# The second batch's first groups leave the start of a two-stage FFT and feed-forward kernel; its first pair loads change queues

## The chip, the cores and the metric

The kernel runs on one core of one Trainium2 chip. The metric is the device time of one execution in microseconds (us). A core has five engines with a queue each: TensorE (PE; weight loads are listed as PEld), VectorE (DVE), ScalarE (ACT), GpSimd (POOL) and SyncE (SP), which here only issues transfers. Transfers are issued by SP, ACT and POOL.

## What is computed

```python
X = np.fft.rfft(x, axis=1)                      # x: 4 batches, 3008 rows, 256 columns
Yr = Xr @ w_r - Xi @ w_i + b_r                  # complex mixing, 256 x 256
Yi = Xr @ w_i + Xi @ w_r + b_i
Yr, Yi = soft_threshold(Yr, 0.01), soft_threshold(Yi, 0.01)
y = np.fft.irfft(Yr + 1j * Yi, n=3008, axis=1)
h = y.reshape(12032, 256) @ w_in                # 256 -> 2048
g = np.maximum(h, 0) + alpha * np.minimum(h, 0)
out = g @ w_out                                 # 2048 -> 256
```

## The kernel before

Each of the four batches goes through four steps, and then through the feed-forward layers. **Step A** is the first half of the transform: 16 groups, each one product over 512 columns in full float32 (`a_mm`, L389) and one copy out of PSUM (`a_evac`, L404 and L406). Batch 0's groups stay in SBUF, in `a0_s`. Those of the other batches are stored to a DRAM buffer `ad` (the L336 issues, made by `put`). **Step B** is the second half: 12 pairs. `b_load` fetches a pair with two transfers of 128 KB into a `bt` tile (three of them), `b_mm` (L428) transforms it with the table `rb_s`, `b_evac` and `b_evac2` split it into a high and a low part (`Xh` by ACT L442, `Xl` by DVE L453, copies by POOL L457), and `m_mm` (L471, L478) applies the mixing weights. **Step C** (`m_evac`, `c_mm`, `c_evac`) is the soft threshold and the first half of the inverse transform, and goes to DRAM (`zd`). **Step D** reads it back (`zt`, L584) and finishes the inverse (L620), which feeds the layers (L689, L726 to L728).

The program is one fixed order, written by hand: each engine takes its instructions in the order in which they are issued, and an instruction that has to wait holds up all that stands behind it on its engine. This goes for SP's transfers too.

The start is: step A of batch 0; four groups of batch 1 (`EARLY`); the loads of the first three pairs, the split of the mixing weights (`split_mix`: high part by ACT, low part by POOL) and the bias parts; `keep_warm(70)`, products on a tile of zeros that keep TensorE busy and whose result nobody reads; then the 12 pairs of batch 0. While the pairs run, `pump` converts feed-forward weights to two-part form with ACT, DVE and POOL: `PT` says how many pieces of this work each pair gets, and `conv_load` fetches the raw weights (`cw_s`, 512 KB each). A list `TAIL` then fills the wait for step C's last stores with ten groups of batch 1 (entries `['f', 4]` and `['f', 6]`, limited by `FILL`).

Then the **weight pass** begins: 48 steps, three chunks of rows for each of the 16 blocks of the hidden layer, while the rest of the weights is converted. What else is to run in a step stands in a table, filled by `at(i, fn, ...)`. The groups of batch 1 that are left go there, by these lines:

```python
for g in range(FILL, NG):
    i = 6 * (g - FILL) + 9
    if g % 2 == 0:
        at(i - 8, a_load, 1, g // 2)
    at(i, a_mm, 1, g)
    at(i, a_evac, 1, g)
```

`a_load` fetches the rows of two groups at once. Also in that table: step 40 loads the table `lc_s` (four transfers of 768 KB, by POOL) and the next `zt`, step 45 loads batch 1's first pair from `ad`, and step 49 (just behind the weight pass) transforms it.

Of the kernel before, what the change touches and what calls it, by code (L numbers as in the profile page):

```python
# [93 lines left out]
def fft_mix_moe(ctx, tc, x, w_r, w_i, b_r, b_i, w_in, w_out, alpha, la, rb, lc, rd, lf, cf, sel, out):  # L94
    nc = tc.nc
# [35 lines left out]
    V, G, A, PE = nc.vector, nc.gpsimd, nc.scalar, nc.tensor  # L131

    def f(t):
        return t.bitcast(F32)

    def split(src, hi, lo, e_hi, e_lo):

        if e_hi is A:
            A.activation(out=hi, in_=src, func=AF.Copy)
        else:  # L140
            e_hi.tensor_copy(out=hi, in_=src)
        e_lo.tensor_tensor(out=lo, in0=src, in1=f(hi), op=ALU.subtract)
# [24 lines left out]
    def half(h):  # L167
        t = const.tile([128, 2, FH * 2 * C], F32R, tag=f"half{h}", name=f"w{h}")
        wi_h[h] = t[:, 0].rearrange("p (w k f) -> p w k f", w=2, k=CT)
        wo_h[h] = t[:, 1].rearrange("p (m w f) -> p m w f", w=2, f=C)  # L170

    def load_tables():
        nc.sync.dma_start(out=rd_s, in_=rd)
        nc.sync.dma_start(out=alpha_s, in_=alpha.rearrange("(k p) -> p k", p=128))
# [33 lines left out]
    def load_mix(*tags):  # L208
        for w, tag in zip((w_r, w_i), tags):
            t = work.tile([128, CT, C], F32, tag=tag, name="wm_f", bufs=1 if tag[1] in "tc" else None)  # L210
            nc.sync.dma_start(out=t, in_=w.rearrange("(k p) f -> p k f", p=128))
            mix_w.append(t)

    def load_rb(n0, n1):
        nc.sync.dma_start(out=rb_s[:, n0:n1], in_=rb[:, n0:n1])
# [9 lines left out]

    def split_mix():
        for t, w in zip(mix_w, mix):
            split(t, w[:, 0], w[:, 1], A, G)
        mix_w.clear()

    def combine_mix():
# [17 lines left out]
    conv_tags = {}  # L249
# [4 lines left out]
    def conv_load():  # L254

        m, i = divmod(conv_m[0], 2)
        conv_m[0] += 1
        k = conv_m[0] % 3
        raw = cw_s[:, NSLOT + 8 * k:NSLOT + 8 * k + 8].rearrange("p (k n) f -> p k (n f)", k=2)
        raw = raw.rearrange("p k (n w) -> p k n w", w=2)  # L260
        src = w_out.bitcast(U32)[256 * m:256 * m + 256] if i else w_in.bitcast(U32)[:, 512 * m:512 * m + 512]
        nc.sync.dma_start(out=raw.rearrange("p k n w -> p k (n w)"), in_=src.rearrange("(k p) f -> p k f", p=128))
        conv_raw.append((raw, m, i))
# [70 lines left out]
    def put(*queues):  # L334
        for n, (o, i) in enumerate(stores):
            (queues or (nc.sync,))[n % max(len(queues), 1)].dma_start(out=o, in_=i)  # L336
        stores.clear()
# [3 lines left out]
    def a_load(b, g):  # L341

        if g == 0:
            ad[b] = dram.tile([NQ, R, C], F32, tag="ad", name=f"ad{b}")
        src = x[b].rearrange("(p r) c -> p r c", r=R)[:, 4 * g:4 * g + 4]
        if b == 0:
            ts = [x_s[:, 4 * g:4 * g + 4]]
        elif b == 1 and g in X1_TAGS:
            tags = X1_TAGS[g]
            ts = [work.tile([NP, 4 // len(tags), C], F32, tag=tag, name="xt", bufs={"Yl": None, "gh": 4}.get(tag, 1))  # L350
                  for tag in tags]
        else:
            ts = [work.tile([NP, 4, C], F32, tag="xt", name="xt")]
        if (b, g) == (0, 0):
            ts = [ts[0][:, 0:2], ts[0][:, 2:4]]
        n = 4 // len(ts)
        for i, t in enumerate(ts):

            for p in ((0, 80), (80, NP)):
                nc.sync.dma_start(out=t[slice(*p)], in_=src[slice(*p), n * i:n * i + n])  # L360
        xt[b, g] = ts

    def x_rows(b, g):
        ts = xt[b, g // 2]
        if len(ts) == 1:
            return [ts[0][:, 2 * (g % 2):2 * (g % 2) + 2]]
        n = len(ts) // 2
        return ts[n * (g % 2):n * (g % 2) + n]
# [13 lines left out]
    def a_mm(b, g):  # L382
        ps = ps_f.tile([NQ, 2, C], F32, tag="f", name="ps_a")
        pa[b, g] = ps
        if b < 2:
            ts = x_rows(b, g)
            n = 2 // len(ts)
            for i, t in enumerate(ts):
                PE.matmul(ps[:, n * i:n * i + n], lf_s, t, start=True, stop=True)  # L389
            return  # L390
        hi, lo = xp.pop((b, g))
        PE.matmul(ps, la_s[:, 0], hi, start=True, stop=False)
        PE.matmul(ps, la_s[:, 1], hi, start=False, stop=False)
        PE.matmul(ps, la_s[:, 0], lo, start=False, stop=True)

    def a_evac(b, g):
        ps = pa.pop((b, g))
        if b == 0:
            st = a0_s[:, g]
        else:  # L400
            tag = A1_TAGS[g] if b == 1 and g < len(A1_TAGS) else "zst"
            st = work.tile([NQ, 2, C], F32, tag=tag, name="ast", bufs={"bt": 3, "zst": 3, "Yt": 1, "Yc": 1}.get(tag))
        if b == 0 and g % 2:
            V.tensor_copy(out=st, in_=ps)  # L404
        else:
            A.activation(out=st, in_=ps, func=AF.Copy)  # L406
        if b:
            stores.append((ad[b][:, 2 * g:2 * g + 2], st))

    bt, xs, xe, yc, ys = {}, {}, {}, {}, {}  # L410

    def b_load(b, q):
        t = work.tile([128, 2, C], F32, tag="bt", name="bt", bufs=3)
        if b == 0:
            src = a0_s.rearrange("(w s q) g r c -> q w s (g r) c", w=4, s=2)[q]
        else:
            src = ad[b].rearrange("(w s q) r c -> q w s r c", w=4, s=2)[q]

        for k in range(2):
            (nc.gpsimd if b == 0 else nc.sync).dma_start(out=t[:, k], in_=src[:, k])  # L420
        bt[b, q] = t

    def b_mm(b, q):
# [548 lines left out]
    MM, M2 = 2, 4  # L972
    PAT = [0, 0] + [1] * 46
    NG = R // 2
    EARLY = 4
    FILL = 14
    C0 = 2
    PT = [1, 2, 3, 3, 3, 3, 3, 3, 3, 3, 4, 4]
    TAIL = [['me', 1], ['ce', 3], ['cm', 2], ['cm', 1], ['ce', 2], ['ce', 1], ['d'], ['f', 4], ['e'], ['f', 6]]
    WARM = 70  # L980
    A1_TAGS = ("zst", "zst", "Yt", "Yc", "bt", "bt", "bt", "Xh", "Xl", "Xh", "Xl", "zst", "zst", "Yc")
    X1_TAGS = {4: ("Yl", "Yl"), 5: ("os", "Yt"), 6: ("gh",) * 4}
    idle = const.tile([128, 128], BF16, name="idle")

    def keep_warm(n):
        ps = ps_f.tile([128, 512], F32, tag="f", name="ps_idle")
        for _ in range(n):
            PE.matmul(ps[:, 0:128], idle, idle, start=True, stop=True)

    with tc.manual_schedule():  # L990
        V.memset(idle, 0.0)
        nc.gpsimd.dma_start(out=lf_s, in_=lf)
        bias_parts = first_bias()
# [2 lines left out]
        for g in range(NG // 2):  # L996
            a_load(0, g)
        load_rb(0, 4)
        for g in range(EARLY // 2):
            a_load(1, g)  # L1000
        load_mix("Yh", "Yh")
        load_rb(4, 12)
        conv_tags.update(v1=("yh", "yl"), ex=("xh", "xh"), lf=("xl", "xl"))
        for _ in range(C0):
            conv_load()
        seq = [(0, g) for g in range(NG)] + [(1, g) for g in range(EARLY)]

        for n, (b, g) in enumerate(seq):
            a_mm(b, g)
            if n >= 1:  # L1010
                a_evac(*seq[n - 1])
            if n == NG:
                for q in range(3):
                    b_load(0, q)
                split_mix()
                bias_parts()
        a_evac(*seq[-1])
        half(0)
        put()
        load_tables()  # L1020
        keep_warm(WARM)

        def run(fn, q, *args):
            if 0 <= q < NPAIR:
                fn(0, q, *args)

        a1 = [EARLY]
        hold = []

        def a_fill(n):  # L1030
            for g in range(a1[0], min(a1[0] + n, FILL)):
                a_mm(1, g)
                a_evac(1, g)
                a1[0] = g + 1

        for t in range(NPAIR + 1):
            run(b_mm, t)
            run(b_load, t + 3)
            run(c_evac, t - 4)
            run(b_evac, t)  # L1040
            run(m_evac, t - 2)
            run(m_mm, t - 1, ps_h)
            run(b_evac2, t)
            run(c_mm, t - 3)
            if t < NPAIR:
                pump(PT[min(t, len(PT) - 1)])
            if t in (2, 5):
                load_rb(2 * t + 8, 2 * t + 14)
            if t < 8 and t % 2 == 0:
                load_cf(3 * t, 3 * t + 6)  # L1050
            if 5 <= t < 10:
                a_load(1, t - 3)
            if t == 10:
                half(1)
                conv_m[1] = FT
# [46 lines left out]
        for b in range(B):  # L1102
# [9 lines left out]
            if b == 0:  # L1112
# [3 lines that stand above are left out]
# [84 lines left out]
        for k in range(len(spairs) + SLAG):  # L1200
# [9 lines left out]
            if k >= SLAG:  # L1210
                n, t = spairs[k - SLAG]
# [43 lines left out]
```

## Time and profile before

| | |
|---|---|
| time, median of 3 runs | 1350.1 us (1348.96 to 1350.62) |
| the profiled execution: its own time | 1350.56 us |
| the profiled execution: span from the first to the last instruction | 1348.8 us |
| TensorE busy | 1335.5 us (99% of the span), 9200 matmul records |
| VectorE, ScalarE, GpSimd busy | 1034.9, 761.0, 375.5 us |
| granted TensorE clock, mean | 0.999 of full speed |

The busy time of TensorE counts the products on zeros as well, so "99% busy" doesn't mean that 99% is useful. A full-float32 product shows as two matmul records. Each view below has the start of an instruction or of a run of instructions in us from the span's start, then its duration.

### The profile page before, as it was taken

Reading aid. Unit: us, or ns where it says so; the run is one execution under the profiler, and the core shown is the slowest. Engines: PE = TensorE matmul, PEld = TensorE weight load, DVE = VectorE, ACT = ScalarE, POOL = GpSimd, SP = SyncE. Lnnn points to the kernel's source line nnn. Section 1 sums busy time; section 2 is a strip of 40 time slices with the busy share of each in tenths; the row PEclk is TensorE's granted clock in tenths of the full one; section 3 lists DMA queues with packets and bytes.
Section 4 is the critical chain, followed back from the end, with each engine's and each line's share of the span. In section 5 each row is a group of like instructions: output and inputs, shape, how many; then the busy total and the mean of one; then the engine's idle time right before and its main releaser. Section 6 shows DMA issues by size and latency. Waiting matters only on the chain.

```text
span 1348.8 us, 25138 instructions
## 1 busy us (share of the span) xinstructions
PE 1335.5 (99%) x9200; PEld 1250.7 (93%) x9200; DVE 1034.9 (77%) x1938; ACT 761.0 (56%) x1526; POOL 375.5 (28%) x400
## 2 busy tenths in 40 slices
PE   8999999999999999999999999999999999999998
PEld 4979999999999999999999999999999999999998
DVE  2767856776777777776768888888888888888885
ACT  3566655665566645555555555655555555555653
POOL 3864642222321222222221211121112111211222
PEclk9999999999999999999999999999999999999999
DMA  9974223342333312111110110111011101110001
GB/s 236 251 202 140 81 94 106 105 138 74 98 115 112 111 54 79 53 51 47 36 36 2 40 28 4 37 28 28 6 35 28 28 6 35 29 28 8 22 17 29
DMA packets 88119, 89.67 MB, mean 66 GB/s; under 512 B 42317, under 2 KB 70448, under 8 KB 87995
## 3 DMA queue, kind: packets, MB, share of 16 engines
q1 hardware_dynamic: 79700, 77.02, 20.1%
q0 software_dynamic: 5168, 8.02, 2.2%
q10 hardware_dynamic: 3127, 3.01, 0.7%
q8 instruction: 73, 1.20, 0.4%
q14 instruction: 51, 0.42, 0.1%
HBM read 50.49 MB, written 34.34 MB: 63 GB/s over the span
## 4 chain that ended last, share of the span: by engine, by line
PE 89%; DVE 3%; DMA 3%; issue 2%; ACT 1%; SPq 1%; POOL 0%; ACTq 0%; DVEq 0%; POOLq 0%
PE ps_h L794 24%; PE ps_h L689 13%; PE ps_m L491 6%; PE ps_o L895 6%; PE ps_o L896 6%; PE ps_o L894 6%; PE ps_d L620 4%; PE ps_o L728 3%; PE ps_o L727 3%; PE ps_o L726 3%; PE ps_b L428 2%; PE o_last L727 1%; PE o_last L728 1%; PE o_last L726 1%; PE o_last L894 1%
## 5 line engine op out<-in xcount | busy, mean ns | idle before, releaser
L794 PE MATMUL ps_h<-yh,w 128*128 128x512 f32 (+1 forms) x960 | 315.6, 389 | 0.0
L833 POOL TENSOR_TENSOR l<-t,h 128x512 fp32r<-128x512 f32 x98 | 127.0, 1296 | 496.5 <-ACT h L831 456.9
L794 PEld LDWEIGHTS ps_h<-yh,w 128*128 128x128 f32 x960 | 180.0, 188 | 33.2
L798 DVE SCALAR_TENSOR_TENSOR sq<-sq,beta_s,ps_h 128x512 f32<-128x512 f32 (+1 forms) x240 | 167.9, 732 | 54.5 <-ACT sq L797 53.6
L689 PE MATMUL ps_h<-yh,w 128*128 128x384 f32 (+1 forms) x704 | 207.0, 337 | 1.3 <-DVE q L696 1.3
L794 PE MATMUL ps_h<-yl,w 128*128 128x512 f32 (+1 forms) x480 | 186.2, 388 | 0.0
L696 DVE SCALAR_TENSOR_TENSOR q<-q,beta_s,ps_h 128x384 f32<-128x384 f32 (+1 forms) x192 | 115.1, 600 | 91.8 <-ACT q L695 90.9
L700 ACT ACTIVATE gh<-q 128x384 fp32r<-128x384 f32 (+1 forms) x192 | 99.1, 516 | 148.0 <-DVE q L696 145.3
L701 POOL TENSOR_TENSOR gl<-q,gh 128x384 fp32r<-128x384 f32 (+1 forms) x90 | 96.8, 1075 | 274.9 <-ACT gh L700 265.4
L813 ACT ACTIVATE dh<-sq 128x768 fp32r<-128x768 f32 x112 | 94.8, 846 | 117.8 <-DVE sq L798 75.8
L797 ACT ACTIVATE sq<-ps_h 128x512 f32<-128x512 f32 (+1 forms) x240 | 133.2, 586 | 26.9 <-PE ps_h L794 25.6
L689 PEld LDWEIGHTS ps_h<-yh,w 128*128 128x128 f32 x704 | 129.3, 189 | 4.4 <-DVE q L696 1.3
L695 ACT ACTIVATE q<-ps_h 128x384 f32<-128x384 f32 (+1 forms) x192 | 91.9, 479 | 62.1 <-PE ps_h L689 61.4
L831 ACT ACTIVATE h<-t 128x512 fp32r<-128x512 f32 x98 | 62.0, 633 | 105.2 <-DVE t L829 103.0
L689 PE MATMUL ps_h<-yl,w 128*128 128x384 f32 (+1 forms) x352 | 116.5, 331 | 0.0
L728 PE MATMUL ps_o<-w,gl 128*128 128x256 f32 x384 | 108.0, 281 | 0.6 <-POOL gl L701 0.6
L727 PE MATMUL ps_o<-w,gh 128*128 128x256 f32 x384 | 107.8, 281 | 0.0
L726 PE MATMUL ps_o<-w,gh 128*128 128x256 f32 x384 | 107.7, 280 | 0.0
L794 PEld LDWEIGHTS ps_h<-yl,w 128*128 128x128 f32 x480 | 90.5, 189 | 13.6
L828 DVE TENSOR_TENSOR dl<-sq,dh 128x768 fp32r<-128x768 f32 x98 | 93.4, 953 | 3.9 <-ACT dh L813 3.9
L896 PE MATMUL ps_o<-l,sw_a 128*128 128x256 f32 x294 | 82.0, 279 | 0.0
L894 PE MATMUL ps_o<-h,sw_a 128*128 128x256 f32 x294 | 81.9, 279 | 0.0
(214 smaller groups left out, 3618.5 us busy)
## 6 DMA issues: line engine op xcount, KB each, us to landing
zt<-zd SPq DMA_DIRECT2D x32, 384.0 KB
zd<-zst SPq DMA_DIRECT2D x37, 256.0 KB
ad<-ast SPq DMA_DIRECT2D x48, 192.0 KB
bt<-ad SPq DMA_DIRECT2D x72, 128.0 KB
xt<-in_x SPq DMA_DIRECT2D x21, 320.0 KB
out<-oT SPq DMA_DIRECT2D x152, 32.0 KB
cw_s<-in_moe_w_in SPq DMA_DIRECT2D x8, 512.0 KB
cw_s<-in_moe_w_out SPq DMA_DIRECT2D x8, 512.0 KB
```

The lines of the kernel that those rows point to most:

```text
L689: PE.matmul(ps, wi_h[m // FH][:, w, ct, 128 * (m % FH):128 * (m % FH) + 128], a[:, ct, 0:n], start=(k == 0), stop=(k == 3 * CT - 1))
L696: V.scalar_tensor_tensor(out=q, in0=q, scalar=beta_s[:, m:m + 1], in1=ps, op0=ALU.mult, op1=ALU.add)
L700: A.activation(out=hi, in_=q, func=AF.Copy)
L726: PE.matmul(a, hi[:, t], w[:, 0], start=(i, k) in first, stop=False)
L727: PE.matmul(a, hi[:, t], w[:, 1], start=False, stop=False)
L728: PE.matmul(a, lo[:, t], w[:, 0], start=False, stop=(i, k) in last)
L794: PE.matmul(ps, wi_h[m // FH][:, w, ct, 128 * (m % FH):128 * (m % FH) + 128], a[:, ct, 0:w1], start=(k == 0), stop=(k == 3 * CT - 1))
L797: A.activation(out=q[:, j], in_=ps, func=AF.Relu, scale=-1.0)
L798: V.scalar_tensor_tensor(out=q[:, j], in0=q[:, j], scalar=beta_s[:, m:m + 1], in1=ps, op0=ALU.mult, op1=ALU.add)
L833: G.tensor_tensor(out=l24, in0=t24, in1=f(h24), op=ALU.subtract)
L894: PE.matmul(o, wh, gh, start=first, stop=False)
L896: PE.matmul(o, wh, gl, start=False, stop=last)
```

## The change

The four early groups of batch 1 are dropped from the start, and with them the loads of their rows and the stores of their results. The tail still does ten groups, now groups 0 to 9 and not 4 to 13; six groups (10 to 15) and not two are left for the weight pass, at steps 9, 15, 21, 27, 33 and 39 and not at 9 and 15. The rows for the tail's groups load with pairs 7 to 11 and not 5 to 9 (and so with two earlier loads). Pairs 0 and 1 of batch 0 are loaded half by SP and half by ACT, ahead of `rb_s` and the raw weights; pair 2 and later ones stay with POOL. The low part of the mixing weights is split by DVE and not by POOL. The two small tables `rd_s` and `alpha_s` load with pair 6 and not before pair 0. `keep_warm(70)` becomes `keep_warm(56)`, and 12 such products come ahead of pair 1. `PT` starts with one piece less in pairs 0 and 1, and has one more in pairs 8 and 9.

```diff
-            split(t, w[:, 0], w[:, 1], A, G)
+            split(t, w[:, 0], w[:, 1], A, V)
...
-    def b_load(b, q):
+    def b_load(b, q, queues=None):
+        queues = queues or ((nc.sync,) * 2 if b else (nc.gpsimd,) * 2)
...
-            (nc.gpsimd if b == 0 else nc.sync).dma_start(out=t[:, k], in_=src[:, k])
+            queues[k].dma_start(out=t[:, k], in_=src[:, k])
...
-    EARLY = 4
-    FILL = 14
+    FILL = 10
-    PT = [1, 2, 3, 3, 3, 3, 3, 3, 3, 3, 4, 4]
+    PT = [0, 1, 3, 3, 3, 3, 3, 3, 4, 4, 4, 4]
-    WARM = 70
+    WARM = 56
...
-        for g in range(EARLY // 2):
-            a_load(1, g)
         load_mix("Yh", "Yh")
+        for g in range(NG):
+            a_mm(0, g)
+            if g:
+                a_evac(0, g - 1)
+        a_evac(0, NG - 1)
+        both = nc.sync, nc.scalar
+        b_load(0, 0, both)
+        b_load(0, 1, both)
         load_rb(4, 12)
+        b_load(0, 2)
         for _ in range(C0):
             conv_load()
-        seq = [(0, g) for g in range(NG)] + [(1, g) for g in range(EARLY)]
...
+        bias_parts()
+        split_mix()
         half(0)
-        put()
-        load_tables()
         keep_warm(WARM)
...
         for t in range(NPAIR + 1):
+            if t == 1:
+                keep_warm(12)
...
-            if 5 <= t < 10:
-                a_load(1, t - 3)
+            if 7 <= t < 12:
+                a_load(1, t - 7)
+            if t == 6:
+                load_tables()
```

SP's queue at the start, behind the last rows of batch 0 (`xt` are rows of batch 1, `wm_f` the mixing weights, `bt<-a_83` halves of pairs 0 and 1, `ad_160` the early groups' stores):

```order
 L215 DMA rb_s<-tab_rb 128x512
-L360 DMA xt<-in_x 80x1024
-L360 DMA xt<-in_x 14x1024
-L360 DMA xt<-in_x 80x1024
-L360 DMA xt<-in_x 14x1024
 L211 DMA wm_f<-in_w_r 128x2x256
 L211 DMA wm_f<-in_w_i 128x2x256
+L421 DMA bt<-a_83 128x1x256 x2
 L215 DMA rb_s<-tab_rb 128x1024
 L262 DMA cw_s<-in_moe_w_in 128x2x512
 L262 DMA cw_s<-in_moe_w_out 128x2x512
-L336 DMA ad_160<-ast 96x512 x4
```

The rows of batch 1 and the stores are gone, and SP's halves of pairs 0 and 1 stand ahead of `rb_s` and of two raw weights.

TensorE's queue in the weight pass at the end of step 21, before the change:

```order
L726 MATMUL ps_o<-w_255,gh 128x256
L727 MATMUL ps_o<-w_255,gh 128x256
L728 MATMUL ps_o<-w_255,gl 128x256
L689 MATMUL ps_h<-Xh,w_255 128x384
L689 MATMUL ps_h<-Xl,w_255 128x384
```

The same place with the change (lines below the new one in the file moved down by one):

```order
L727 MATMUL ps_o<-w_232,gh 128x256
L728 MATMUL ps_o<-w_232,gh 128x256
L729 MATMUL ps_o<-w_232,gl 128x256
L389 MATMUL ps_a<-xt,lf_s 96x512
L690 MATMUL ps_h<-Xh,w_232 128x384
L690 MATMUL ps_h<-Xl,w_232 128x384
```

One group of step A stands between the second layer's products of one step and the first layer's of the next; so it is at steps 27, 33 and 39 too.

SP's queue ahead of batch 1's first pair (`bt<-ad`), before the change, from the last store of a group (`ad_160<-ast`) on:

```order
L336 DMA ad_160<-ast 96x512
L262 DMA cw_s<-in_moe_w_in 128x2x512
L262 DMA cw_s<-in_moe_w_out 128x2x512
L211 DMA wm_f<-in_w_r 128x2x256
L211 DMA wm_f<-in_w_i 128x2x256
L181 DMA bias<-in_b_r 128x256
L181 DMA bias<-in_b_i 128x256
L584 DMA zt<-zd_495 96x1024
L420 DMA bt<-ad_160 128x1x256 x2
```

And with the change:

```order
L336 DMA ad_719<-ast 96x512 x2
L211 DMA wm_f<-in_w_r 128x2x256
L211 DMA wm_f<-in_w_i 128x2x256
L181 DMA bias<-in_b_r 128x256
L181 DMA bias<-in_b_i 128x256
L336 DMA ad_719<-ast 96x512
L585 DMA zt<-zd_460 96x1024
L421 DMA bt<-ad_719 128x1x256 x2
```

The last store, that of step 39's group, now stands directly ahead of the `zt` load for step 45 and of batch 1's first pair.

## Rows read from the trace of the kernel before

**Rows 1.** The page: busy us, share of the span and records of each engine.
```profile
PE 1335.5 (99%) x9200; PEld 1250.7 (93%) x9200; DVE 1034.9 (77%) x1938; ACT 761.0 (56%) x1526; POOL 375.5 (28%) x400
```

**Rows 2.** Timeline of TensorE, start: start us, duration us, instructions, idle before.
```profile
25.52 4.07 PE L988 MATMUL ps_idle<-idle 128*128 128x128 bf16 x70
30.42 1.80 PE L428 MATMUL ps_b<-rb_s,bt 128*128 128x128 f32 x12 [0.83 <-issue]
...
33.56 0.47 PE L471 MATMUL ps_m<-bias_p,ones 128*128 128x512 f32 x1
...
36.72 1.05 PE L428 MATMUL ps_b<-rb_s,bt 128*128 128x128 f32 x8
```

**Rows 3.** Timeline of the other engines around the first pair loads.
```profile
19.94 0.69 DVE L404 COPY a<-ps_a 96x512 f32<-96x512 f32 x1 [1.03 <-PE ps_a L389]
...
20.27 0.37 SPq L262 DMA_DIRECT2D cw_s<-in_moe_w_out  x1
...
21.29 4.11 POOL L420 DMA_DIRECT2D bt<-a  x6 [16.19 <-DVE bias_h L201]
```

**Rows 4.** Tile `bt`, issue to landing: the load issued at 21.3, then 18 to 60 us.
```profile
DMA to landing us min/median/max: 9.0/9.0/9.0
...
DMA to landing us min/median/max: 4.2/8.5/9.9
```

**Rows 5.** Transfers of the first 100 us: issues, KB each, us from issue to landing.
```profile
lf_s<-tab_lf POOLq DMA_DIRECT2D x1, 35.2 KB, 2.9
```

**Rows 6.** Chain of work that ended last, in order of time: start, duration, what.
```profile
17.30 6.10 DMA wm_f<-in_w_i
...
92.09 8.59 PE ps_a L389 x24
...
206.56 0.89 PE ps_b L428 x8
```

**Rows 7.** Stages: length, busy time of PE, PEld, DVE, ACT, POOL, clock, DMA, GB/s.
```profile
4.70:20.70 16.00, 14.81 (x36) 5.03 (x34) 5.56 (x11) 4.74 (x8) 0.40 (x1) 1.00 1.06 231
20.70:25.50 4.80, 3.69 (x8) 1.19 (x9) 1.15 (x3) 2.71 (x5) 4.11 (x6) 1.00 1.07 356
...
50.00:70.00 20.00, 20.00 (x153) 19.25 (x152) 17.34 (x23) 11.94 (x22) 19.30 (x24) 1.00 1.03 278
```

**Rows 8.** Timelines: `Xl` of pairs 10 and 11 on VectorE, its first use on TensorE.
```profile
79.19 0.67 DVE L453 TENSOR_TENSOR Xl<-ps_b,Xh 128x512 fp32r<-128x512 f32 x1
...
84.50 0.68 DVE L453 TENSOR_TENSOR Xl<-ps_b,Xh 128x512 fp32r<-128x512 f32 x1
...
79.54 1.05 PE L428 MATMUL ps_b<-rb_s,bt 128*128 128x128 f32 x8
...
74.70 1.05 PE L428 MATMUL ps_b<-rb_s,bt 128*128 128x128 f32 x8
...
85.23 0.39 PE L478 MATMUL ps_m<-wr_s,Xl 128*128 128x256 f32 x1
```

**Rows 9.** Timeline of SP: the last row loads of batch 1 with pair 9.
```profile
70.24 9.29 SPq L360 DMA_DIRECT2D xt<-in_x  x12
```

**Rows 10.** Timeline of TensorE in the weight pass: its idle gaps from 150 us on.
```profile
151.15 0.44 PE L689 MATMUL ps_h<-Xh,w 128*128 128x384 f32 x1 [0.38 <-DVE q L696]
...
159.71 0.44 PE L689 MATMUL ps_h<-yh,w 128*128 128x384 f32 x1 [0.39 <-DVE q L696]
...
168.99 0.39 PE L728 MATMUL ps_o<-w,gl 128*128 128x256 f32 x1 [0.62 <-POOL gl L701]
```

**Rows 11.** A stage behind these gaps (columns as in rows 7).
```profile
170.00:180.00 10.00, 10.00 (x75) 10.00 (x74) 6.09 (x12) 5.23 (x13) 5.29 (x4) 1.00 0.00 0
```

**Rows 12.** Tile `ast`, 100 to 150 us: ScalarE's copies, ns min/median/max.
```profile
L406 ACT ACTIVATE ast<-ps_a x4: 576/586/594, 99.9 to 138.0; 96x512 f32<-96x512 f32 x4
```

**Rows 13.** Timelines of SP and GpSimd ahead of batch 1's first pair.
```profile
149.30 1.28 SPq L420 DMA_DIRECT2D bt<-ad  x2
...
187.41 2.96 POOL L224 DMA_DIRECT2D lc_s<-tab_lc  x4
```

More of the change, by code (lines that the diff above doesn't have):

```diff
@@ L974, in fft_mix_moe @@
     NG = R // 2
-    EARLY = 4
-    FILL = 14
+    FILL = 10
     C0 = 2
-    PT = [1, 2, 3, 3, 3, 3, 3, 3, 3, 3, 4, 4]
+    PT = [0, 1, 3, 3, 3, 3, 3, 3, 4, 4, 4, 4]
     TAIL = [['me', 1], ['ce', 3], ['cm', 2], ['cm', 1], ['ce', 2], ['ce', 1], ['d'], ['f', 4], ['e'], ['f', 6]]
-    WARM = 70
-    A1_TAGS = ("zst", "zst", "Yt", "Yc", "bt", "bt", "bt", "Xh", "Xl", "Xh", "Xl", "zst", "zst", "Yc")
-    X1_TAGS = {4: ("Yl", "Yl"), 5: ("os", "Yt"), 6: ("gh",) * 4}
+    WARM = 56
+    A1_TAGS = ("bt", "bt", "bt", "Xh", "Xl", "Xh", "Xl", "zst", "zst", "Yc")
+    X1_TAGS = {2: ("Yl", "Yl"), 3: ("os", "Yt"), 4: ("gh",) * 4}
     idle = const.tile([128, 128], BF16, name="idle")
@@ L998, in fft_mix_moe @@
         load_rb(0, 4)
-        for g in range(EARLY // 2):
-            a_load(1, g)
         load_mix("Yh", "Yh")
+        conv_tags.update(v1=("yh", "yl"), ex=("xh", "xh"), lf=("xl", "xl"))
+        for g in range(NG):
[6 more added lines that the diff above has]
+        b_load(0, 1, both)
         load_rb(4, 12)
-        conv_tags.update(v1=("yh", "yl"), ex=("xh", "xh"), lf=("xl", "xl"))
+        b_load(0, 2)
         for _ in range(C0):
             conv_load()
-        seq = [(0, g) for g in range(NG)] + [(1, g) for g in range(EARLY)]
[L1008 to L1017, printed above, removed]
+        bias_parts()
+        split_mix()
         half(0)
-        put()
-        load_tables()
         keep_warm(WARM)
@@ L1025, in run @@
                 fn(0, q, *args)
-        a1 = [EARLY]
+        a1 = [0]
         hold = []
```

## The prediction

> **What bounds the kernel now.** I read the page first: TensorE is busy for 1335.5 us of the span of 1348.8 us [rows 1], so the time is TensorE's own work plus its gaps. The change removes no useful product. It can pay only by shortening the time in which TensorE does nothing useful, and the page hides the largest such place, since products on zeros count as busy. The timeline of TensorE at the start shows it: between the four early groups of batch 1 and pair 0 stand 4.07 us of products on zeros, the first pair's transform comes only at 30.42, and the first mixing product at 33.56 [rows 2]. Once the pairs run TensorE has no gap (20.00 us busy of 50 to 70, at a granted clock of 1.00 [rows 7]), so what is won ahead of 33.56 moves all that follows, unless a later stage gives it back.
>
> What holds back 30.42? The last group of step A is out of PSUM at 19.94 + 0.69 = 20.63, and GpSimd issues six loads from 21.29 on [rows 3]. The first landed 9.0 us later [rows 4], at 30.3. So the wait is for pair 0's load. That load was behind others: a 512 KB raw weight was issued one microsecond ahead [rows 3], the mixing weight landed at 17.30 + 6.10 = 23.40 [rows 6], and the transfer engines were busy throughout (share 1.07 [rows 7]).
>
> **Pairs 0 and 1 by SP and ScalarE, and nothing ahead of them.** They can be issued at 20.63. The rows of batch 1 (two loads of 384 KB, 768 KB) no longer stand ahead of the mixing weights; at the 231 GB/s of that stage [rows 7] this is 3.3 us, so the weights land at about 20.1 and the queue is then empty. `rb_s` and the raw weights are issued behind. How long a load of this kind takes from these queues no row shows. From below: a 35 KB load by GpSimd into a quiet chip took 2.9 us [rows 5]. From above: 9.0 us as now. The two halves of a pair bring 256 KB, 0.7 us at 356 GB/s [rows 7]. As the queue is empty I take the near end, 3.4 us: pair 0's transform starts at 24.0. The 56 products on zeros end before that (from 19.94, when the last group is being copied out, 56/70 of 4.07: 23.2).
>
> Then come the transform (1.05 [rows 2]), 12 products on zeros (12/70 of 4.07 = 0.70) and pair 1's transform (1.05). The first mixing product is at 26.8 and not at 33.56: **6.8 us earlier**. The ends are 7.6 (landing right with the zeros' end) and 1.2 (9.0 us to land). Of 4.07 us of zeros 3.26 and 0.70 stay; their change costs nothing while they lie within the wait for a load. The mixing weights' low parts move to VectorE, which is idle then; two operations of some 0.7 us, as its `Xl` [rows 8], end some 2 us ahead of the first mixing product, and GpSimd is free earlier. The small tables `rd_s` and `alpha_s` are read only behind the tail, five pairs and more after their new place, so they cost nothing.
>
> **Pairs 2 and 3 by GpSimd.** Mixing of pair 0 takes 36.72 - 33.56 = 3.16 us [rows 2], so pair 2 is wanted at 30.0, its second half at 30.5. Its second load is issued some 0.7 us behind 20.63; with the longest landing seen, 9.9 us [rows 4], it is there at 31.2. Pair 3's can be issued only when pair 0's transform has freed a tile, at 25.1, and is wanted four microseconds behind pair 2; with 9.9 us its second half is 1 us late. So 0 to 1.3 us of new stalls. The early stores (four of 192 KB) and the rows have left this stretch, which argues for less: I take **0.4**.
>
> **The conversion pieces.** With four pieces in a pair, `Xl` of pair 11 starts 5.31 us behind that of pair 10, while the pair period is 4.84 us; it ends at 85.18, and TensorE's product that reads it starts at 85.23, with no slack [rows 8]. The new `PT` has more pairs of four, so VectorE could be late from pair 9 on. But the pieces done by the end of pair 7, 8, 9 and 10 are 19, 23, 27, 31, and were 21, 24, 27, 31: never more. Where VectorE carries a backlog, it is no worse; where it doesn't, two pieces of about 1 us are bunched at the end. 0 to 1 us, I take **0.2**.
>
> **The later row loads.** The last of the early ones ended its issue at 70.24 + 9.29 = 79.53 [rows 9]. Two pairs later this is 89.2 on the old clock. The tail's ninth group, which reads it, comes at 92.09 + 8 x 0.86 = 99.0 [rows 6]. Ten microseconds cover it; without that cover, each late microsecond would cost one.
>
> **Four more groups in the weight pass.** Ten groups take 8.59 us in the tail [rows 6], 0.86 each, so four add **3.4 us** of TensorE work where it had hardly a gap. Some of it falls into gaps: the three from 150 us on are 0.38, 0.39 and 0.62 [rows 10], where TensorE waits for VectorE and GpSimd. The groups at steps 21 and 27 give those engines 1.7 us more, so up to 1.4 us is absorbed; behind 170 us TensorE has no gap [rows 11], and the groups at steps 33 and 39 cost their full 1.7. ScalarE's four copies of 0.59 us [rows 12] run beside the next step's first-layer products and on an engine half busy [rows 11]; without that cover they would cost up to 2.3 more. Cost 2.0 to 3.4; I take **2.6**.
>
> **SP in the weight pass.** The store of step 39's group now holds up SP, and behind it `zt` for step 45 and batch 1's first pair. That pair was issued at 149.30 and wanted at 206.56 [rows 6, 13], 56 us of cover; now it has about 18, in which the four `lc_s` loads issued from 187.41 on run [rows 13]. If store and load land in under 9 us each, it costs nothing.
>
> **The sum.** 6.8 - 0.4 - 0.2 - 2.6 = 3.6 us less. On the profiled execution's 1350.56 (span 1348.8 and 1.76 around it) this is 1346.96; that execution stood 0.46 above the median of 1350.1, so the forecast is **1346.5 us**.
>
> **Rivals.** *The pair lands as late as before* (slower). What made the load slow was then not what stood ahead of it, but the transfer itself and those that share the transfer engines. Landing 9.0 us behind 20.63 puts the first mixing product at 32.4, 1.2 us earlier and no more. Behind it stand the same 0.4, 0.2 and 2.6: 2.0 us slower, 1352.1; with 1.3, 1.0 and 3.4 it is 1354.6. It decides from a landing later than 27.2 (6.6 us), where the start wins only the 3.2 that the rest costs. For it speaks that every load of a pair took 4.2 us or more [rows 4]; against it, that the engines' queue is drained by then. TensorE would also stand idle for six microseconds; the rows show a clock of 1.00 with gaps below one [rows 2, 7] and nothing for so long a gap, so a fall of the clock would come on top. I give it 0.08.
>
> The Trainium skill, "DMA: Bandwidth & Descriptors", section "Issuing engines are not separate DMA queues", speaks against the change of queue: transfers of all issuing engines run on the same 16 transfer engines, and several issuers save only the time to issue. By that rule alone the landing would be near 29.6 and the time near 1352.1. The trace shows the shared engines full in that stretch, as the rule says; but the change also takes away what they were full of, and on this my sum rests.
>
> *The start's gain is eaten by the next loads.* Pairs 2 and 3 late by 1.3 us together, VectorE by 1.0, and the weight pass at its full 3.4: 6.8 - 5.7 = 1.1, so 1349.0, no change that can be told. For it: the landings of 8.5 us in the middle [rows 4]. 0.22.
>
> *Batch 1 starts late.* The store of step 39's group goes out at about 187.9, lands 9.9 us later, then the pair's two issues (1.28 [rows 13]) and 9.9 us more: 209.0, and TensorE stalls for 2.4 us at 206.56. Result 1348.9. Against it: the stores and loads there share the engines with `lc_s` for some 9 us only. 0.08.
>
> *The forecast*, a gain of 2.7 to 5.5 us: 0.62.
>
> **Chances and range.** A measurement of this kernel tells about 0.2%, 2.7 us, from no change. Faster (below 1347.4): 0.61, the forecast's chance less a little for its upper edge. Within: 0.32, from the second and third rival and half of the first. Slower: 0.07, the other half and mishaps not named. The range for 8 in 10 is 1344.5 to 1349.8: its lower end is a start of 7.6 with no stall and 2.0 for the weight pass, its upper the second rival with some of the first; the forecast's own is 1344.5 to 1347.4.
>
> **What would show it.** In the profile of the changed kernel: the first transform of a pair near 24, the first mixing product near 26.8; gaps of at most half a microsecond ahead of pairs 2 and 3; the pair period still 4.84; the tail's groups starting some 6.2 us earlier than 92.09; the gaps of rows 10 smaller; batch 1's first transform 3.6 us earlier than 206.56 and no wait for `bt` there. I am wrong if the first mixing product comes behind 29, if pairs 2 to 4 wait for their loads by more than 1.3 us, or if the weight pass grows by more than 3.4 us.

## The result, and the profile after

The changed kernel takes 1361.01 us (median of 6 runs, 1360.13 to 1362.33) against 1350.36 for before (6 runs): 1.0079 times, 95% interval 1.0066 to 1.0092. That is **slower by about 10.6 us, where 3.6 less had been forecast**. The profiled execution took 1361.67 us, with a span of 1359.3.

TensorE's row of the page, after (busy us, share, records):

```profile
PE 1339.0 (99%) x9198; PEld 1255.0 (92%) x9198; DVE 1035.1 (76%) x1940; ACT 760.5 (56%) x1526; POOL 369.0 (27%) x394
```

Its busy time is up by only 3.5 us of the 10.5 [rows 1]: most of the loss is idle time. TensorE's timeline at the start, after, as in [rows 2]:

```profile
19.85 3.29 PE L988 MATMUL ps_idle<-idle 128*128 128x128 bf16 x56
28.06 2.05 PE L429 MATMUL ps_b<-rb_s,bt 128*128 128x128 f32 x8 [4.92 <-DMA bt<-a]
29.89 1.49 PE L988 MATMUL ps_idle<-idle 128*128 128x128 bf16 x12
34.55 0.68 PE L429 MATMUL ps_b<-rb_s,bt 128*128 128x128 f32 x4 [3.17 <-DMA bt<-a]
37.07 1.22 PE L429 MATMUL ps_b<-rb_s,bt 128*128 128x128 f32 x4 [1.83 <-DMA bt<-a]
37.94 0.77 PE L472 MATMUL ps_m<-bias_p,ones 128*128 128x512 f32 x1
...
43.07 1.05 PE L429 MATMUL ps_b<-rb_s,bt 128*128 128x128 f32 x8
```

Pair 0's transform is 2.4 us earlier than before, not 6.4. Then TensorE waits for each half of pair 1 in turn (3.17 and 1.83), and the first mixing product comes 4.38 us *later* than before. Pair 0's mixing then takes 5.13 us (37.94 to 43.07) where it took 3.16. Its products last 0.63 and 0.41 us, not 0.40 and 0.28. The windows say why (columns as in [rows 7]):

```profile
20.70:25.50 4.80, 2.44 (x44) 2.27 (x41) 2.54 (x7) 1.15 (x2) 1.43 (x2) 0.98 0.43 98
25.50:30.40 4.90, 2.34 (x13) 2.31 (x14) 0.00 (x0) 0.26 (x1) 0.00 (x0) 0.50 1.03 228
30.40:40.00 9.60, 4.60 (x26) 4.07 (x24) 1.39 (x2) 1.49 (x3) 4.08 (x8) 0.68 0.88 220
40.00:50.00 10.00, 10.00 (x76) 9.92 (x76) 3.45 (x7) 3.57 (x7) 5.24 (x10) 0.88 0.38 113
```

After idle stretches of 4.92, 3.17 and 1.83 us TensorE runs at its lower level (0.50, 1.2 GHz) until about 42 us. And in the first window, while the pairs' loads are pending, the transfer engines are busy for a share of only 0.43, at 98 GB/s; before it was 1.07 and 356. So the prediction's empty queue came true (the mixing weights had landed by 19.2), and the loads were slow in it.

Further on, the chain of work that ended last, in order of time:

```profile
22.01 15.01 DMA bt<-a
...
77.72 7.62 DMA cw_s<-in_moe_w_out
...
100.62 8.60 PE ps_a L389 x24
...
217.37 0.89 PE ps_b L429 x8
```

Between pair 2's transform and the tail's groups stand 57.55 us (43.07 to 100.62), before 55.37; from there to batch 1's first transform 116.75 and 114.47 [rows 2, 6]; from there to the end of the span 1141.93 and 1142.24. So 4.38 (start) + 1.97 (slow clock) + 2.18 (pair stage) + 2.28 (weight pass) - 0.31 = 10.5.

### The profile page after: what moved, and what is told of

It is laid out like the page before. It is cut to its first block, busy times and chain, and to the rows that moved or that the text cites. A ratio compares the mean times of both kernels' runs of the same rounds, so it can differ in the third digit from the quotient of the medians.

```text
span 1359.3 us, 25132 instructions
## 1 busy us (share of the span) xinstructions
PE 1339.0 (99%) x9198; PEld 1255.0 (92%) x9198; DVE 1035.1 (76%) x1940; ACT 760.5 (56%) x1526; POOL 369.0 (27%) x394
## 4 chain that ended last, share of the span: by engine, by line
PE 92%; DMA 3%; DVE 2%; ACT 1%; issue 1%; SPq 0%; ACTq 0%; DVEq 0%
PE ps_h L795 24%; PE ps_h L690 14%; PE ps_m L492 6%; PE ps_o L896 6%; PE ps_o L897 6%; PE ps_o L895 6%; PE ps_d L621 4%; PE ps_o L729 3%; PE ps_o L728 3%; PE ps_o L727 3%; PE ps_b L429 3%; PE ps_a L389 2%; PE o_last L728 1%; PE o_last L729 1%; PE o_last L727 1%; PE o_last L895 1%
```

## The experiments

In each table row: median of the run, ratio to before with its interval, start of the first mixing product, of the tail's groups and of batch 1's first transform, by TensorE's timeline. The last two differences separate the stages. The starts are those of one profiled execution, whose own time can lie up to 2.2 us from the run's median (v3_pair0: 1351.73), so the stages do not always add up to the difference of the medians.

| run | us | ratio (95%) | mixing | tail | batch 1 | mixing to tail | tail to batch 1 |
|---|---|---|---|---|---|---|---|
| before | 1350.4 to 1351.0 | | 33.56 | 91.92 | 206.40 | 58.36 | 114.48 |
| changed | 1361.01 | 1.0079 (1.0066 to 1.0092) | 37.94 | 100.46 | 217.20 | 62.52 | 116.74 |
| e1_pool | 1355.55 | 1.0034 (1.0020 to 1.0047) | 33.60 | 95.15 | 212.23 | 61.55 | 117.08 |
| e3_split | 1355.19 | 1.0035 (1.0019 to 1.0051) | 32.91 | 93.97 | 211.04 | 61.06 | 117.07 |
| e4_warm | 1358.92 | 1.0062 (1.0039 to 1.0085) | 36.67 | 97.92 | 215.00 | 61.25 | 117.08 |
| e5_hold | 1356.16 | 1.0044 (1.0029 to 1.0060) | 32.59 | 95.38 | 212.19 | 62.79 | 116.81 |
| e2_queue_alone | 1360.78 | 1.0074 (1.0057 to 1.0091) | 42.83 | 102.27 | 216.71 | 59.44 | 114.44 |
| e6_tables | 1355.09 | 1.0034 (1.0022 to 1.0046) | 35.43 | 95.14 | 212.01 | 59.71 | 116.87 |
| e7_rows | 1357.01 | 1.0050 (1.0035 to 1.0065) | 33.54 | 95.46 | 212.35 | 61.92 | 116.89 |
| e8_pt | 1353.17 | 1.0019 (1.0009 to 1.0029) | 33.37 | 91.98 | 209.03 | 58.61 | 117.05 |
| e9_after_pt | 1360.24 | 1.0076 (1.0061 to 1.0090) | 37.96 | 98.85 | 215.72 | 60.89 | 116.87 |
| e10_wide | 1352.60 | 1.0017 (1.0005 to 1.0028) | 30.92 | 92.27 | 209.06 | 61.35 | 116.79 |
| v3_pair0 | 1353.92 | 1.0024 (1.0014 to 1.0034) | 32.22 | 90.88 | 207.66 | 58.66 | 116.78 |
| v2a_sp_act | 1352.98 | 1.0015 (1.0006 to 1.0024) | 32.74 | 92.42 | 206.87 | 59.68 | 114.45 |
| v2b_sp | 1351.60 | 1.0004 (0.9995 to 1.0013) | 31.43 | 93.77 | 208.20 | 62.34 | 114.43 |
| v4a | 1359.00 | 1.0063 (1.0051 to 1.0075) | 32.88 | 101.52 | 215.93 | 68.64 | 114.41 |
| v4b | 1358.30 | 1.0060 (1.0047 to 1.0073) | 30.80 | 99.41 | 213.82 | 68.61 | 114.41 |
| v5a | 1355.62 | 1.0035 (1.0023 to 1.0047) | 32.68 | 94.92 | 209.69 | 62.24 | 114.77 |
| v5b | 1354.30 | 1.0027 (1.0016 to 1.0038) | 32.23 | 95.34 | 210.13 | 63.11 | 114.79 |
| v5c | 1357.80 | 1.0043 (1.0030 to 1.0057) | 31.27 | 99.64 | 214.45 | 68.37 | 114.81 |

**The start.** In the expectations, theory 1 says that such a load, which reads four partitions, is slow in itself, theory 2 that the traffic behind slows it, and theory 3 that the queues of SP and ScalarE are slow for it, whatever its shape.

e1_pool, the changed kernel with both pairs on GpSimd:

```diff
-        b_load(0, 0, both)
-        b_load(0, 1, both)
+        b_load(0, 0)
+        b_load(0, 1)
```

> The changed kernel, but pairs 0 and 1 loaded by GpSimd as before. Theory 1 (a pair's load, read from four partitions, uses only a few of the 16 transfer engines when SP or ScalarE issue it) and theory 3 (these two queues are slow for it, whatever its shape): the first mixing product comes near 34 and not at 37.9, about 1357 us. Theory 2 (the table and raw weights issued right behind hold the pairs back, whoever issues them): pair 1 is as late as in the changed kernel, 37 to 38, and the time stays near 1361.

The start is back where it was before (33.60), with the same traffic cleared and the same loads behind: the 4.4 us hang on the queues that issue the pairs. GpSimd's loads read the same four partitions, and yet pair 1 has landed at 31.1, not at 37.0. Its queue shows them as packets of 4 KB, the other two as packets of 1 KB; why they get through earlier is not shown. The rest of the loss remains.

e2_queue_alone, the kernel before with the queues of pairs 0 and 1 alone:

```diff
-                    b_load(0, q)
+                    b_load(0, q, (nc.sync, nc.scalar) if q < 2 else None)
```

> The kernel before with one part of the change: pairs 0 and 1 loaded by SP and ScalarE, pair 2 by GpSimd, everything else as before (two early groups of the second batch, tables first, 70 zeros). Theory 1 (the loss at the start belongs to the queues: these loads are slow on SP and ScalarE and share the transfer engines with what SP has issued behind them): pair 1 lands some 4 us later than before, the first mixing product moves from 33.6 to about 37 to 38 us, and the time is 1354 to 1357 us. Theory 2 (the queues are fine by themselves, the loss comes from the other parts that stand at the same place): first mixing product at 31 to 33.6 us, time 1348 to 1351 us.

This one edit costs as much as the whole change, and puts mixing even later than expected, for a reason that no theory had listed. Timelines of ScalarE and TensorE:

```profile
20.83 10.60 ACTq L421 DMA_DIRECT2D bt<-a  x2
31.47 0.63 ACT L139 ACTIVATE wr_s<-wm_f 128x512 fp32r<-128x512 f32 x1 [11.68 <-DMA bt<-a]
...
33.16 2.02 PE L389 MATMUL ps_a<-xt,lf_s 94*96 94x512 f32 x2 [9.65 <-ACT ast L406]
```

From the start of ScalarE's first issue to the end of its second there are 10.6 us (1.74 in the changed kernel), and the early groups' copies behind them held up TensorE. The issues themselves take 1.17 and 0.55 us. The second one goes out at 30.88, because it waits for the semaphore that tells of the first load's landing: here the program gives both loads the same semaphore, and its last update by the first load comes at 30.86. In the changed kernel the two loads have different ones. The first load landed 10 us after its issue, with two raw weights issued by SP just ahead of it. So the size of this loss has a cause of its own, and the run does not price the queues alone.

e3_split, each half as four transfers, one for each source partition:

```diff
+            if split4:
+                for w in range(4):
+                    queues[k].dma_start(out=t[32 * w:32 * w + 32, k], in_=src[w:w + 1, k])
...
-        b_load(0, 0, both)
-        b_load(0, 1, both)
+        b_load(0, 0, both, True)
+        b_load(0, 1, both, True)
```

> The changed kernel, but each half of pairs 0 and 1 is fetched by four transfers, one for each source partition, with 32 rows each; same queues, same bytes, four times the issues. Theory 1: all transfer engines take part, pair 0 lands near 25 and pair 1 near 28; first mixing product near 29, the clock hardly falls, about 1350 us. Theory 2: the traffic behind is the same, pair 1 still lands at 34 to 37, about 1361 us. Theory 3: no better than 1361, rather worse by the added issues.

Pair 0 is no earlier (28.34), pair 1 is (31.46). Neither falls where a theory had put it. In 20.70 to 25.50 the share is 0.46 and the rate 63 GB/s: more engine time, not more bytes. But the edit brings a limit of its own: the eight issues of a queue now last 7.5 us (ScalarE) and 7.8 us (SP), and 512 KB in 7.8 us are 67 GB/s, about what was moved. So the run does not tell slow reading from slow issuing.

e5_hold takes the traffic away: table slices and raw weights behind pair 3, which is on SP and ScalarE too.

```diff
-        load_rb(4, 12)
         b_load(0, 2)
-        for _ in range(C0):
-            conv_load()
...
-            run(b_load, t + 3)
+            run(b_load, t + 3, *((both,) if t == 0 else ()))
+            if t == 0:
+                load_rb(4, 12)
+                for _ in range(C0):
+                    conv_load()
```

> The changed kernel, but the second part of the table and the first two raw weights are issued by SP only behind pair 3's load, which SP and ScalarE issue here and which waits for pair 0's transform. So nothing but pair 2 shares the transfer engines with pairs 0 and 1. Theory 2: pair 1 lands by 29, first mixing product near 30, about 1352 us, unless the raw weights are then late. Theory 1: the four halves still go through a few engines one after the other, some 2 to 2.7 us each from 22.4 on, pair 1 lands at 31 to 33 and the time is 1354 to 1357. Theory 3: 36 or later, 1360.

Its windows:

```profile
20.70:25.50 4.80, 2.82 (x51) 2.64 (x48) 2.92 (x7) 1.15 (x2) 1.43 (x2) 1.00 0.26 65
25.50:30.40 4.90, 2.84 (x18) 2.81 (x19) 0.00 (x0) 0.22 (x1) 0.00 (x0) 0.72 0.31 85
```

Alone on the chip, the loads of three pairs use about a quarter of the transfer engines' time, at 65 to 85 GB/s. Pair 0 lands at 27.56, half a microsecond earlier than with the traffic; pair 1 at 31.7 and not 37.1. Traffic costs pair 1 some 5 us; pair 0 is slow by itself. The kernel gains less than that (1356.16), as the table slices and raw weights are then late in their turn: pair 2's transform waits 1.29 us for `rb_s`.

e10_wide keeps queues, bytes and packets and reads from 64 partitions, not 4 (pairs 0 and 1 then hold other rows than the reference's):

```diff
+            if b == 0 and q < 2:
+                wide = a0_s[32 * k:32 * k + 64, R // 2 - 1]
+                queues[k].dma_start(out=t[:, k], in_=wide)
```

> The changed kernel with the same two loads on the same queues at the same place, the same 128 packets of 1 KB in each half, but read from 64 partitions of the operand (its last group's slab) and not from 4; pairs 0 and 1 hold other rows, so these two pairs' results are not the reference's. Theory 1 (what makes these loads slow is that a half is read from 4 partitions, for which few transfer engines run): pair 0's first transform at 23 to 25 us, pair 1 landed by 26, first mixing product at 26 to 28 us, share of the transfer engines in 20.7 to 25.5 above 0.8. Theory 2 (it is the queues, or the traffic behind): pair 0 at 27 to 28.5 us, pair 1 at 34 to 37, first mixing product at 37 to 38 us as in the changed kernel.

TensorE's timeline:

```profile
23.99 1.13 PE L433 MATMUL ps_b<-rb_s,bt 128*128 128x128 f32 x8 [0.46 <-ACT wi_s L139]
24.96 0.83 PE L992 MATMUL ps_idle<-idle 128*128 128x128 bf16 x12
29.57 1.70 PE L433 MATMUL ps_b<-rb_s,bt 128*128 128x128 f32 x8 [3.78 <-DMA bt<-a]
30.92 0.77 PE L476 MATMUL ps_m<-bias_p,ones 128*128 128x512 f32 x1
```

Pair 0's transform starts at 23.99, at the predicted 24.0, and no longer waits for its load at all. Its halves landed 2.7 and 3.2 us after their issue. So for pair 0 it is the source: theory 1, and not theory 3, since the queues are the same. Pair 1 still lands behind the expected 26, at 29.57, beside raw weights and slices issued from 22.5 us on: there theory 2 has its part. The share of the first window was 0.50, not above 0.8.

e4_warm fills the idle time with 250 products on zeros:

```diff
-    WARM = 56
+    WARM = 250
```

> The changed kernel with 250 products on zeros and not 56 ahead of pair 0, so that TensorE is busy to about 34.4. All theories of the load leave the first mixing product near 38. If the fall of the clock to half cost the difference between 5.1 us (pair 0's mixing now) and 3.2 us (before), the time falls by about 2.0, to 1359; if the clock cost nothing that counts, it stays at 1361.

The zeros now hold pair 0 back to 33.83, and the clock stays up; the window of 30.4 to 40 us:

```profile
30.40:40.00 9.60, 9.51 (x120) 9.26 (x118) 1.38 (x2) 1.75 (x3) 4.62 (x9) 1.00 0.81 218
```

Pair 0's mixing takes 3.15 us (36.67 to 39.82) where the changed kernel took 5.13: the clock term is 2.0. That the whole kernel also takes 2.1 us less agrees in part by luck, since mixing starts 1.27 us earlier here too and later stages give about as much back.

**The pair stage.** With the start of before, e1_pool still loses 3.2 us between mixing and tail. Theory A: the loads moved into that stage make raw weights late. Theory B: four conversion pieces in pairs 8 to 11 are too many. All three runs start from e1_pool.

```diff
 e6_tables
         half(0)
+        load_tables()
...
-            if t == 6:
-                load_tables()
 e7_rows
-            if 7 <= t < 12:
-                a_load(1, t - 7)
+            if 5 <= t < 10:
+                a_load(1, t - 5)
 e8_pt
-    PT = [0, 1, 3, 3, 3, 3, 3, 3, 4, 4, 4, 4]
+    PT = [1, 2, 3, 3, 3, 3, 3, 3, 3, 3, 4, 4]
```

> The changed kernel with pairs 0 and 1 on GpSimd (which gave 1355.6 us, its start as before, 3.2 us lost between pair 0 and the last pairs), and with the two table loads back ahead of pair 0. Theory A (the table loads, whose second one is of 4-byte pieces, and the row loads at pairs 7 to 11 make the raw weights late in the pair stage): if the tables are the cause, the tail's first filling group moves from 95.3 to about 92 to 93 us and the time to 1352.5 to 1353.5 us. Theory B (the pieces per pair, four in pairs 8 to 11 instead of three): no change, 1355 to 1356 us.

> The changed kernel with pairs 0 and 1 on GpSimd, and with the five row loads of the second batch at pairs 5 to 9 instead of 7 to 11. Theory A with the row loads as the cause: the tail's first filling group moves from 95.3 to 92 to 93.5 us, time 1352.5 to 1354 us. Theory A with the tables, or theory B (the pieces): no change, 1355 to 1356 us.

> The changed kernel with pairs 0 and 1 on GpSimd, and with the pieces per pair of before (1, 2, 3 ... 3, 4, 4 instead of 0, 1, 3 ... 3, 4, 4, 4, 4; both are 35). Theory B (four pieces in pairs 8 to 11 are what slows them): the tail's first filling group moves from 95.3 to 92 to 93 us, time 1352.5 to 1353.5 us. Theory A (late raw weights by the loads around them): no change or a little slower, as the pieces are then wanted earlier, 1355 to 1357 us.

e8_pt gets all of it back (58.61 against before's 58.36), e7_rows nothing. e6_tables misses its expectation in the total and at the tail (95.14), because the tables ahead of the pairs make mixing start 1.8 us later and at the lower clock. Behind that it does get the loss back: from pair 2's transform to the tail it takes 55.69 us, where e1_pool takes 58.39, e8_pt 55.46 and the kernel before 55.20. How both can be right shows in e1_pool's timelines of SP, ScalarE, VectorE and TensorE:

```profile
60.67 0.56 SPq L174 DMA_DIRECT2D alpha_s<-in_moe_alpha  x1
...
65.23 0.39 SPq L262 DMA_DIRECT2D cw_s<-in_moe_w_in  x1
...
75.62 0.69 ACT L275 ACTIVATE conv<-cw_s 128x512 f32<-128x512 f32 x1 [2.05 <-DMA cw_s<-in_moe_w_in]
...
80.60 0.60 ACT L443 ACTIVATE Xh<-ps_b 128x512 fp32r<-128x512 f32 x1 [2.72 <-POOL w L294]
81.09 0.68 ACT L505 ACTIVATE Yc<-ps_m,lam_s 128x512 f32<-128x512 f32 x1
...
81.81 0.69 DVE L506 SCALAR_TENSOR_TENSOR Y<-ps_m,Yc 128x512 f32<-128x512 f32 x1 [2.46 <-ACT Yc L505]
...
82.55 0.50 PE L472 MATMUL ps_m<-bias_p,ones 128*128 128x512 f32 x1 [1.48 <-DVE Y L506]
```

A raw weight issued at 65.23, behind the tables, lands 10 us later; the same one lands after 6.9 us in e6_tables. How the tables delay it is not shown: `alpha_s` itself has landed at 65.9. The conversion piece that reads it holds up ScalarE for 2.05 us; `Xh`, `Yc`, `Y` and TensorE's next product come late behind it, and with four pieces in every pair there is no room to catch up. Take either cause away and that wait is gone: in e6_tables and e8_pt no piece on ScalarE (L275) waits for a raw weight in this stage; in the changed kernel, e1_pool and e7_rows one waits 1.8 to 2.1 us. It takes both: in v3_pair0 below, with the old `PT`, a piece waits 1.80 us for a late raw weight, and mixing to tail is still 58.66.

e9_after_pt makes e8_pt's edit in the changed kernel itself:

> The changed kernel whole, with only the pieces per pair put back to those of before (1, 2, 3 ... 3, 4, 4). If the loss in the pair stage is the four pieces in pairs 8 to 11 meeting a late raw weight (as the run with both pairs on GpSimd showed), the 2.2 us between the third pair and the tail come back and the start and the weight pass stay as they are: 1358.5 to 1359.5 us. Rival: with the start this late the pieces have other partners, nothing comes back: 1360.5 to 1361.5 us.

Mixing to tail falls by 1.6 us in the profiled execution, most of this term. The median falls by 0.8, to a ratio of 1.0076 where it was 1.0079, with intervals that overlap: between the two expectations, and too little to be told from no change.

**Better versions.** If two pairs on one route follow each other, pair 0 on the hardware queues and pair 1 on GpSimd might run side by side. v3_pair0 does so from e8_pt with 100 zeros. v2a_sp_act does it in the kernel before, with the early groups kept; v2b_sp has both halves on SP:

```diff
 v3_pair0 (against e8_pt)
-    WARM = 56
+    WARM = 100
-        b_load(0, 0)
+        b_load(0, 0, both)
 v2a_sp_act (against before; v2b_sp has nc.sync twice)
-        load_rb(4, 12)
-        for _ in range(C0):
-            conv_load()
...
-                for q in range(3):
-                    b_load(0, q)
+                b_load(0, 0, (nc.sync, nc.scalar))
+                load_rb(4, 12)
+                for _ in range(C0):
+                    conv_load()
+                b_load(0, 1)
+                b_load(0, 2)
```

> The changed kernel with the pieces of before, only pair 0 on SP and ScalarE, pairs 1 and 2 on GpSimd, and 100 zeros instead of 56. Theory (the two loads on SP and ScalarE follow each other on few transfer engines; one pair there and one on GpSimd run side by side): pair 0 lands at about 27.6 us, pair 1 at about 29.5, first mixing product at 30.5 to 31.5 us against 33.6, clock at 1.00; the weight pass still costs 2.6 us: 1350 to 1351.5 us. Rival (what limits a pair's load is its source, or the traffic beside it, whichever queue it is on): first mixing product at 33 us or later, 1352.5 to 1354 us.

> The kernel before with one thing of the change: pair 0 alone on SP and ScalarE, its issue ahead of the remaining table slices and the first raw weights, pairs 1 and 2 on GpSimd; the four early groups stay. Theory: first mixing product at 30.5 to 31.5 us instead of 33.6, time 1347.5 to 1349.5 us. Rival (ScalarE's issue holds up its evictions of the early groups, as with the queue change alone, where two issues stood for 10.6 us and TensorE waited 9.65 us): 1352 us or more.

> The same as the run of the kernel before with pair 0 on SP and ScalarE, but both halves on SP. Theory (the halves follow each other on either queue): as that run within 1 us, without any hold of ScalarE, 1347.5 to 1349.5 us. Rival (two halves on one queue take twice as long as on two): pair 0 lands 1.5 to 2 us later than with both queues, 1349.5 to 1351 us.

Mixing starts 0.8 to 2.1 us earlier than before, but none of the three is faster. v3_pair0 pays 2.3 us in the weight pass. The other two lose the gain in the pair stage; v2b_sp's longest such wait, on ScalarE:

```profile
45.81 0.68 ACT L275 ACTIVATE conv<-cw_s 128x512 f32<-128x512 f32 x1 [3.91 <-DMA cw_s<-in_moe_w_in]
```

v4a and v4b (from v2a_sp_act and v2b_sp) let that raw weight go first, by moving stores and tables; v5a and v5b move only the tables, and v5c (from v5b) loads a third raw weight ahead of the stores:

```diff
 v4a, v4b; v5a, v5b without the three lines on put()
-        put()
-        load_tables()
...
+            if t == 2:
+                put()
+            if t == 6:
+                load_tables()
 v5c
-    C0 = 2
+    C0 = 3
```

> The kernel before with pair 0 on SP and ScalarE ahead of table slices and raw weights, pairs 1 and 2 on GpSimd, and with SP's four stores of the second batch's early groups moved behind pair 2 and the two table loads behind pair 6. Theory (with pair 0 alone moved, the start was 0.8 us earlier and 1.3 us were lost where a late raw weight met the pieces; without stores and tables in front, the third raw weight is issued at 25 us instead of 33): first mixing product at 31.5 to 32.5 us, pair stage as before, 1347.5 to 1350 us. Rival (stores and tables only collide with something later): 1350.5 to 1353 us.

> As the run with SP and ScalarE, with both halves of pair 0 on SP. Theory: first mixing product at 31 to 32 us, pair stage as before, 1347.5 to 1349.5 us, faster than before by 0.1 to 0.2%. Rival: 1350.5 to 1352.5 us.

> The kernel before with pair 0 on SP and ScalarE ahead of table slices and raw weights, pairs 1 and 2 on GpSimd, and the two table loads behind pair 6; the stores of the early groups stay where they were (moved behind pair 2 they held up a tile that the combination of pair 0 writes, 6.8 us). Theory (the third raw weight, late behind stores and tables, is what ate the earlier start): it is issued at about 30 instead of 33 us, the pair stage takes 54.4 to 55 us instead of 55.7, 1347.5 to 1350 us. Rival (the stores' traffic alone makes it late): 1350 to 1353 us.

> As the run with SP and ScalarE, with both halves of pair 0 on SP. Theory: first mixing product at 31 to 32 us, pair stage 54.4 to 55 us instead of 57.6, 1347.5 to 1349.5 us. Rival: 1350.5 to 1352 us.

> As the run with both halves of pair 0 on SP and the tables behind pair 6, with the third raw weight issued ahead of the four stores. Theory: the third raw weight is there before its first piece, first mixing product at 31 to 32 us, 1347.5 to 1349 us. Rival (with three raw weights in front, pair 1 and the stores come later by as much): 1350.5 to 1354 us.

All five miss. In v4a and v4b `Yc` of pair 0 shares a buffer with an early group's result, and waits for its store (v4a, ScalarE):

```profile
44.55 0.69 ACT L505 ACTIVATE Yc<-ps_m,lam_s 128x512 f32<-128x512 f32 x1 [6.78 <-DMA ad<-ast]
```

In v5a to v5c the third raw weight does go earlier (29.14 in v5a against 33.28 in v2a_sp_act), but later ones are then late where tables and rows now meet them (waits of ScalarE of 0.5 to 2.1 us between 64 and 79 us), and in v5b pair 3's load is late too. No version tried beats before; v2b_sp equals it.

## Why the prediction was wrong, point by point

- **The start** (forecast 6.8 us earlier, measured 4.4 later) is the step that failed: "The two halves of a pair bring 256 KB, 0.7 us at 356 GB/s [rows 7]. As the queue is empty I take the near end, 3.4 us." In place of 3.4 us pair 0 took 7.2 (issued at 20.82, used at 28.06), and pair 1's second half 15.0. The 356 GB/s came from loads spread over many partitions. A half reads 4 partitions, and e5_hold shows 65 to 85 GB/s for such loads with nothing else beside them. e10_wide shows that the remaining steps of the term were sound: with another source pair 0's transform starts at 23.99. That it meets the predicted 24.0 so closely is luck, as the issue came 0.5 us later than predicted and the last wait there is for ScalarE's `wi_s`. The upper end failed too: 9.0 us was a row for pair 0, taken as a bound for both. Pair 1's second half was issued by 22.6 and used at 37.07, with the traffic that the change puts behind these loads running beside it. Of the 14.1 us between forecast and measurement the start is 11.2, the clock 2.0 and the pair stage 1.6; the rest is 0.6 the other way.
- **The rival "the pair lands as late as before"** had the kind right: the transfer itself and those that share the engines. Its price was wrong, because it let pair 1 land with pair 0. Its limit of 27.2 should be 27.6 by its own numbers (24.0 + 6.8 - 3.2); pair 0 was used at 28.06, behind either. Its fall of the clock came, and cost 2.0 us; it was named without a price.
- The Trainium skill's rule weighed there ("DMA: Bandwidth & Descriptors", section "Issuing engines are not separate DMA queues") says that several issuers save only the time to issue. It was right that the change of queue gains nothing, but it does not give the loss: e1_pool, with GpSimd's loads, starts mixing 4.3 us earlier than the changed kernel, and the time came out above the 1352.1 worked out beside it.
- **Pairs 2 and 3** (0.4): no wait for pair 2 at 43.07; with the start that late it was not put to the test.
- **The conversion pieces** (0.2, at most 1; measured 2.2): "never more" counted pieces done by the end of a pair, but not when raw weights for them arrive. **The tables** ("they cost nothing") named who reads them and not what is issued behind them on SP. Each alone costs little (from pair 2's transform to the tail 0.3 us with the tables moved, 0.5 with the pieces moved), both together 2.2 to 3.2 us.
- **The row loads** (nothing): right, as e7_rows shows no gain from the old place.
- **The weight pass** (2.6): right; measured 2.28. All kernels with six groups there take 116.7 to 117.1 us from tail to batch 1, all with two 114.4 to 114.8. From 140 to 215 us the gaps of [rows 10], with one of 0.25 more, were 1.64 us; two are left, 0.24 and

```profile
168.69 0.45 PE L690 MATMUL ps_h<-yh,w 128*128 128x384 f32 x1 [0.37 <-DVE q L697]
```

  so 1.0 us of the four groups' 3.4 was absorbed. The SP step was right too: batch 1's first pair is issued at 199.14, 18 us ahead of its use, with no wait.

A better forecast was within reach: 4.2 us as the shortest landing of any pair [rows 4], and four source partitions in the code, spoke for a slow load; the trace of before could not price pair 1.

## What to carry to other kernels

Price a transfer by a row with the same source and destination pattern, not by the stage's GB/s: here four source partitions cost 4 us for pair 0 and 7.5 for pair 1 (the changed kernel against e10_wide), where the bytes are worth 0.7. When a load is moved ahead, name what is now issued behind it and next to it, and what every queue behind it feeds; two small tables ahead of a weight cost 2 to 3 us here, once the engine that waits for the weight had no slack. If a wait for data can last microseconds at the start, price the clock for the work behind it.

## What the runs showed of the hardware

- A half of 128 KB, read from 4 partitions, took about a quarter of the transfer engines. In the changed kernel the two halves of pair 0, issued at the same time on two queues, went one after the other: ScalarE's landed at 25.1, SP's at 27.9. The transfer queues of 22 to 24 us (q10 is ScalarE's, q1 SP's; packets, MB, share):

```profile
q10 hardware_dynamic: 124, 0.13, 22.0%
...
q1 hardware_dynamic: 10, 0.01, 1.4%
```

  The Trainium skill, "DMA: Bandwidth & Descriptors", section "Why a DMA increments its semaphore by 16 and not by 1", says that a transfer uses as many engines, up to 16, as divide the slowest dimensions of both sides, and on these queues always the lowest-numbered ones. For 4 and 128 that is 4 of 16, the same four for both halves. The shares of 0.22 and 0.26 agree. So do the updates of the semaphore that tells of a landing: as the data land there are four for a half in the changed kernel, and 16 in e10_wide (64 and 128: 16). For e3_split's quarters (32 and 32) the rule gives 16 as well, and there are 16; pair 0 was no earlier all the same, but its issues were slow too. So the number of source partitions is shown as the cause; whether by the engines' number or by reading few partitions stays open.
- An issue can seem to stand for 10.6 us although no queue holds it (e2_queue_alone): ScalarE's second load waited for the semaphore of its first, which landed 10 us after its issue, and all of ScalarE's work stood behind it.
